# The first two units of a chunked attention kernel: another load order, other PSUM banks, and one hand-over at a time

## The chip, the core and the metric

The kernel runs on one core of a Trainium2 chip. The metric is device time in microseconds (us) of one execution. Six parts matter here: PE (TensorE, matrix multiplies), DVE (VectorE), ACT (ScalarE), POOL (GpSimd), SP (SyncE, which here only issues DMA transfers) and the DMA engines. Each engine works through its own list of instructions in order, and semaphores tie the lists together.

## What is computed

A linear attention with a decaying state, per batch and head, and behind it two feed-forward layers:

```
for t in range(S):                                    # S = 768, D = 48, 4 batches, 8 heads
    y[:, :, t] = r_t @ (state + (u * k_t) v_t)
    state      = w_t[:, None] * state + k_t v_t
x   = y as [3072 tokens, 384]
x   = max(x @ w_in, 0) ** 2 @ w_out                   # 384 -> 2048 -> 384
out = ((x @ w_a) * (x @ w_b)) @ w_out2                # 384 -> 1536 -> 384
```

## The kernel before

The 768 steps are cut into 6 chunks of 128, so that there are 24 units (a chunk of one batch), numbered chunk by chunk. For a unit, `load_unit` fetches four tiles: `lw` (decays), `lkr` (k and r, transposed), `vn` (v) and `nn` (k and r with tokens on partitions). `prepare` turns decays into factors on DVE (two scans at L197 and L202, four products at L206 to L210), while POOL multiplies `nn` with `u` (tile `u_bc`) and with itself (L220, L221); DVE sums that up to `dd` (L223), and ACT builds a diagonal `A` from it (L226, eight instructions). `scores` lets PE multiply k with r into two PSUM tiles `ps` (L239, four matmuls each) and transpose k into `pt` (L243); its `post` copies the scores over `A` under a mask on DVE (L247, two copies) and takes `pt` out on ACT (L250). `mix` lets PE multiply `A` with v into `py` (L267) and k with v into `pk` (L274); its `post` copies `py` to SBUF on ACT (L284), shifts it with six small DMAs (L287) and updates the state on DVE (L292, L294).

Units 0 and 1 make the first tile of tokens, 256 wide. The first layer then runs over it in 16 steps (L414): three matmuls into `hp` (L417), a relu on ACT (L423), a product on DVE (L424, tile `g`), and, two steps later, three matmuls into `acc` (L410). `hp` has two PSUM buffers, so that the third `hp` step waits for the first product. Weights come packed: `decode` takes two ACT and two DVE instructions a tile (L41 to L44), and `split_w1` parts the decoded tile into a high and a low half for the later, 512 wide tiles (L144, L145). In those each step is nine matmuls into `hp` and nine into `acc` (L311 to L313), with a product at L464 and a split at L372 on DVE. The attention of later units, the decoding and the splits run between these steps.

The program's text is not the order in which the engines work. A scheduler builds each engine's list from the data that instructions need, from priorities and from its own timeline; `high_priority(offset=HP)` pulls work ahead. So an edit to the first two units moves instructions of other units too. PSUM's eight banks are in three pools: `p_acc` (3, the layer's sums), `p_mm` (2, `hp`) and `p_at` (3, attention).

Of the kernel before, what the change touches and what calls it, by code (L numbers as in the profile page):

```python
# [8 lines left out]
F32 = mybir.dt.float32  # L9
# [7 lines left out]
B, H, S, D = 4, 8, 768, 48  # L17
# [3 lines left out]
C = 128  # L21
# [3 lines left out]
G = 4  # L25
GP = 112
T = B * C
HP = 100
# [43 lines left out]
def chunked_path(ctx, tc, flags, krT, wT, krn, vn, u, w1, w2, w3, w4, w5, out):  # L72
    nc = tc.nc
    pe, act, dve, pool, sync = nc.tensor, nc.scalar, nc.vector, nc.gpsimd, nc.sync
# [8 lines left out]
    at = ctx.enter_context(tc.tile_pool(name="at", bufs=1))  # L83
    dr = ctx.enter_context(tc.tile_pool(name="dr", bufs=1, space=bass.MemoryType.DRAM))
    p_acc = ctx.enter_context(tc.tile_pool(name="p_acc", bufs=3, space=PS))
    p_mm = ctx.enter_context(tc.tile_pool(name="p_mm", bufs=2, space=PS))
    p_at = ctx.enter_context(tc.tile_pool(name="p_at", bufs=3, space=PS))
# [82 lines left out]

    loaded = {}

    def load_unit(i):
        b, c = units[i]
        w = ld.tile([GP, G * (C + 1) + 1], F32, tag="lw", name="lw")
        kr = ld.tile([GP, 2, G, C], F32, tag="lkr", name="lkr")
        v = ld.tile([128, H, D], F32, tag="vn", name="vn", bufs=3)
        nn = ld.tile([128, 2, H, D], F32, tag="nn", name="nn")
        r0 = b * S + c * C
        sync.dma_start(out=w, in_=wT[b, c])  # L180
        sync.dma_start(out=kr, in_=krT[b, c])
        sync.dma_start(out=v, in_=vn[r0:r0 + C].rearrange("p (h d) -> p h d", h=H))
        sync.dma_start(out=nn, in_=krn[r0:r0 + C].rearrange("p n (h d) -> p n h d", h=H))
        loaded[i] = w, kr, v, nn

    xt = {}
    tiles = [(0, 1)] + [tuple(range(i, i + 4)) for i in range(2, NU - 2, 4)] + [(NU - 2, NU - 1)]
# [3 lines left out]
    def prepare(i):  # L191
        b, c = units[i]
        w, kr, v, nn = loaded.pop(i)
        k, r = kr[:, 0], kr[:, 1]
        fq = at.tile([GP, 2, G * (C + 1)], F32, tag="f", name="fq")
        f, q = (fq[:, n].rearrange("p (g t) -> p g t", g=G) for n in range(2))
        dve.tensor_tensor_scan(  # L197
            out=fq[:, 0], data0=w[:, :-1], data1=d1.rearrange("p g t -> p (g t)"),
            initial=0.0, op0=ALU.mult, op1=ALU.max,
        )  # L200
        dve.reciprocal(out=d2[:, :, C:], in_=f[:, :, C:])
        dve.tensor_tensor_scan(  # L202
            out=fq[:, 1, ::-1], data0=w[:, 1:][:, ::-1], data1=d2.rearrange("p g t -> p (g t)")[:, ::-1],
            initial=0.0, op0=ALU.mult, op1=ALU.add,
        )
        dve.tensor_tensor(out=r, in0=r, in1=f[:, :, 0:C], op=ALU.mult)  # L206
        e = w[:, 0:G * C].rearrange("p (g t) -> p g t", g=G)
        dve.tensor_tensor(out=k, in0=k, in1=q[:, :, 1:], op=ALU.mult)
        dve.tensor_tensor(out=e, in0=f[:, :, 1:], in1=q[:, :, 1:], op=ALU.mult)
        dve.scalar_tensor_tensor(  # L210
            out=k, in0=e, scalar=2.0, in1=k, op0=ALU.subtract, op1=ALU.mult, reverse0=True
        )
        pe2 = at.tile([GP, G, 2, 1], F32, tag="pe2", name="pe2", bufs=2)
        dve.tensor_tensor(
            out=pe2[:, :, :, 0], in0=f[:, :, C:C + 1].to_broadcast([GP, G, 2]),
            in1=half.to_broadcast([GP, G, 2]), op=ALU.mult,
        )
        act.activation(out=fq, in_=fq, func=AF.Square, accum_out=chk[:, i:i + 1])
        p = nn[:, 0]
        pool.tensor_tensor(out=p, in0=p, in1=u_h, op=ALU.mult)  # L220
        pool.tensor_tensor(out=p, in0=p, in1=nn[:, 1], op=ALU.mult)  # L221
        dd = at.tile([128, H, 1], F32, tag="dd", name="dd", bufs=2)
        dve.tensor_reduce(out=dd[:, :, 0], in_=p, axis=AX.X, op=ALU.add)  # L223
        A = at.tile([128, 2, G, C], F32, tag="A", name="A", bufs=2)
        for h in range(H):
            act.activation(out=A[:, h % 2, h // 2, :], in_=ident, func=AF.Copy, scale=dd[:, h])  # L226
        unit[i] = dict(k=k, r=r, v=v, A=A, pe2=pe2)
        if i + 2 < NU:
            load_unit(i + 2)

    def scores(i):

        b, c = units[i]
        st = unit[i]
        ps = [p_at.tile([128, G, C], F32, tag="at", name="ps") for _ in range(2)]
        for g in range(G):
            for j in range(2):
                s = slice(64 * j, 64 * j + D)
                pe.matmul(out=ps[j][:, g, :], lhsT=st["k"][s, g, :], rhs=st["r"][s, g, :], start=True, stop=True)  # L239
        if c < NC - 1:  # L240
            pt = p_at.tile([128, 4, C], F32, tag="at", name="pt")
            for g in range(G):
                pe.transpose(out=pt[:, g, 0:GP], in_=st["k"][:, g, :], identity=ident[:GP, :GP])  # L243

        def post():
            for j in range(2):
                dve.copy_predicated(st["A"][:, j], mask.bitcast(I32).to_broadcast([128, G, C]), ps[j])  # L247
            if c < NC - 1:
                st["kt"] = at.tile([128, G, GP], F32, tag="kt", name="kt")
                act.activation(out=st["kt"], in_=pt[:, :, 0:GP], func=AF.Copy)  # L250
        return post

    def mix(i):

        b, c = units[i]
        st = unit.pop(i)
        A, v, s = st["A"], st["v"], states[b]
        ps = p_at.tile([128, G, C], F32, tag="at", name="py")
        if c > 0:
            for g in range(G):  # L260
                pe.matmul(
                    out=ps[0:GP, g, :], lhsT=s[:, g].rearrange("p j d -> p (j d)")[:, 0:GP],
                    rhs=st["r"][:, g, :], start=(g == 0), stop=False, skip_group_check=True,
                )
        for g in range(G):
            for j in range(2):
                pe.matmul(  # L267
                    out=ps[64 * j:64 * j + D, g, :], lhsT=v[:, 2 * g + j, :], rhs=A[:, j, g, :],
                    start=(c == 0), stop=True, skip_group_check=True,
                )  # L270
        if c < NC - 1:
            pk = p_at.tile([128, G, 2, D], F32, tag="at", name="pk")
            for g in range(G):
                pe.matmul(out=pk[0:GP, g], lhsT=st["kt"][:, g, :], rhs=v[:, 2 * g:2 * g + 2, :], start=True, stop=True)  # L274

        def post():
            if i > 1:
                x = at.tile([128, G, C], F32, tag="x", name="xf", bufs=2)
            else:
                if i == 0:  # L280
                    x0[0] = xp.tile([128, G, 2, C], F32, tag="x", name="x0")
                x = x0[0][:, :, i, :]
            for rows in ((slice(0, GP),) if c > 0 else (slice(0, D), slice(64, GP))):
                act.activation(out=x[rows], in_=ps[rows], func=AF.Copy)  # L284
            for p0 in (0, 64):
                for m in range(3):
                    sync.dma_start(out=x[p0 + 48:p0 + 64, m], in_=x[p0 + 16 * m:p0 + 16 * m + 16, 3])  # L287
            if c < NC - 1:
                src = pk[0:GP]
                if c > 0:  # L290
                    t = at.tile([GP, G, 2, D], F32, tag="kt", name="t")
                    dve.tensor_tensor(out=t, in0=src, in1=s[:, :, :, 0:D], op=ALU.add)  # L292
                    src = t
                dve.tensor_tensor(  # L294
                    out=s[:, :, :, 0:D], in0=src, in1=st["pe2"].to_broadcast([GP, G, 2, D]), op=ALU.mult
                )
            return (lambda: split_x(i, x)) if i > 1 else None
        return post
# [14 lines left out]
        pe.matmul(out=out, lhsT=wt[:, 1, sl], rhs=rhs_hi, start=False, stop=last)  # L313


    load_unit(0)
    make_identity(nc, ident)
    for s in states:
        pool.memset(s, 0.0)
# [2 lines left out]
        out=mask, in_=mask, pattern=[[0, 1], [1, 128]], compare_op=ALU.is_gt, fill=0.0, base=0, channel_multiplier=-1  # L322
# [7 lines left out]
    dve.memset(half[0:64, :, 0:1], 1.0)  # L330
    dve.memset(half[64:GP, :, 1:2], 1.0)
    sync.dma_start(out=u_bc, in_=u.rearrange("h d -> (h d)").rearrange("(o n) -> o n", o=1).to_broadcast([128, DM]))
    load_unit(1)
    load_w1(2)
    tails = []
    with tc.high_priority(offset=HP):
        prepare(0)
    for i in range(2):
        with tc.high_priority(offset=HP):
            p = scores(i)  # L340
            if i == 0:
                prepare(1)
            p()
            mix(i)()
        decode_w1()
        decode_w1()

# [56 lines left out]
    acc = [p_acc.tile([128, N], F32, tag="acc", name="acc") for _ in range(3)]  # L404
# [9 lines left out]
    for f in range(16):  # L414
        hp = p_mm.tile([128, N], F32, tag="mm", name="hp")
        for k in range(3):
            pe.matmul(  # L417
                out=hp, lhsT=w_in[f][:, k * 128:(k + 1) * 128],
# [22 lines left out]
    for n in range(1, len(tiles)):  # L441
# [4 lines left out]
        acc = [p_acc.tile([128, N], F32, tag="acc", name="acc") for _ in range(3)]  # L446
# [281 lines left out]
```

## Time and profile before

| | us |
|---|---|
| median of 3 runs (lowest to highest) | 1030.02 (1028.35 to 1032.36) |
| the profiled execution | 1029.76 |
| its span in the trace | 1028.1 |
| PE busy | 984.1 (96%) |
| DVE busy | 540.5 (53%) |
| ACT busy | 448.3 (44%) |
| POOL busy | 72.7 (7%) |

The span is 1.66 us shorter than the execution's own time. PE is busy in 96% of the span, so 44.0 us are all that its idle time comes to. The shares of the whole span hide where that lies: the page's 40 slices, the waits and the timeline of the first 260 us tell it. A busy PE is not a PE at full speed: the duration of a matmul of one shape has to be looked at beside it.

### The profile page before, as it was taken

To read this page: it belongs to the slowest core of one execution; us is meant where nothing else is said; L and a number is where in the kernel's file an instruction comes from. 1 tells how busy PE (TensorE), PEld (TensorE's weight loads), DVE (VectorE), ACT (ScalarE), POOL (GpSimd) and SP (SyncE) were. 2 spreads that over 40 slices of the span, in tenths; PEclk is the share of its full clock that TensorE was granted. 3 is DMA by queue.
4 is the path that set the end of the run, shared out by engine and by line. 5 is a ranking of instruction groups with operands and counts; after the bars stand their busy time and mean duration, and the time that the engine had idled before them with its cause. 6 is when DMAs were issued, how large, how long until landed. Compare 5 with 4: busy or idle time off the path is not lost. (4 is left out here: it accounts for less than half of the span.)

```text
span 1028.1 us, 13834 instructions
## 1 busy us (share of the span) xinstructions
PE 984.1 (96%) x5250; PEld 834.4 (81%) x5250; DVE 540.5 (53%) x908; ACT 448.3 (44%) x930; POOL 72.7 (7%) x60
## 2 busy tenths in 40 slices
PE   3789999998999999999999999999999999999996
PEld 2577777777788888887889988888888888888885
DVE  8999999988856756644346622222222222222221
ACT  5788676777555444543336612222322312212211
POOL 4234201000100100000000000000000000000000
PEclk9999999999999999999999999999999999999998
DMA  9677237877422221201015400100100100000001
GB/s 274 218 254 244 67 95 254 258 257 244 146 83 64 77 67 54 65 21 54 23 46 155 132 1 2 61 1 21 41 1 1 41 1 16 27 1 32 0 1 34
DMA packets 47020, 88.15 MB, mean 86 GB/s; under 512 B 7008, under 2 KB 25568, under 8 KB 46944
## 3 DMA queue, kind: packets, MB, share of 16 engines
q1 hardware_dynamic: 40464, 77.74, 24.5%
q10 hardware_dynamic: 6480, 9.44, 2.6%
q8 instruction: 43, 0.70, 0.3%
q14 instruction: 33, 0.27, 0.1%
HBM read 69.46 MB, written 16.52 MB: 84 GB/s over the span
## 5 line engine op out<-in xcount | busy, mean ns | idle before, releaser
L536 DVE TENSOR_TENSOR t<-ap,t 128x512 f32<-128x512 f32 x72 | 49.8, 691 | 278.7 <-PE ap L313 278.7
L371 ACT ACTIVATE gh<-t 128x512 fp32r<-128x512 f32 (+1 forms) x168 | 102.4, 609 | 185.3 <-DVE t L536 127.0
L372 DVE TENSOR_TENSOR gl<-t,gh 128x512 fp32r<-128x512 f32 (+1 forms) x168 | 112.1, 667 | 74.7 <-ACT gh L371 74.4
L527 ACT ACTIVATE t<-bp 128x512 f32<-128x512 f32 x72 | 43.1, 598 | 160.4 <-PE bp L313 159.7
L311 PE MATMUL hp<-x,w 128*128 128x512 f32 (+1 forms) x288 | 109.3, 379 | 2.7 <-DVE t L464 2.7
L312 PE MATMUL acc<-gl,w 128*128 128x512 f32 (+1 forms) x288 | 108.2, 376 | 1.9 <-DVE gl L372 1.8
L313 PE MATMUL acc<-gh,w 128*128 128x512 f32 (+1 forms) x288 | 107.5, 374 | 0.0
L312 PE MATMUL hp<-x,w 128*128 128x512 f32 (+1 forms) x288 | 107.2, 372 | 0.0
L313 PE MATMUL hp<-x,w 128*128 128x512 f32 (+1 forms) x288 | 107.1, 372 | 0.0
L311 PE MATMUL acc<-gh,w 128*128 128x512 f32 (+1 forms) x288 | 102.6, 383 | 0.0
L464 DVE TENSOR_TENSOR t<-t,hp 128x512 f32<-128x512 f32 (+1 forms) x96 | 61.0, 635 | 74.0 <-ACT t L463 74.0
L518 PE MATMUL acc<-w,gh 128*128 128x384 f32 x288 | 96.8, 336 | 0.0
L519 PE MATMUL acc<-w,gh 128*128 128x384 f32 x288 | 96.7, 336 | 0.0
L520 PE MATMUL acc<-w,gl 128*128 128x384 f32 x288 | 95.1, 337 | 0.0
L463 ACT ACTIVATE t<-hp 128x512 f32<-128x512 f32 (+1 forms) x96 | 53.3, 555 | 83.2 <-PE hp L313 81.3
L313 PE MATMUL bp<-x,w 128*128 128x512 f32 x216 | 85.3, 395 | 0.0
L312 PE MATMUL bp<-x,w 128*128 128x512 f32 x216 | 85.1, 394 | 0.0
L312 PE MATMUL ap<-x,w 128*128 128x512 f32 x216 | 84.1, 390 | 0.0
L313 PE MATMUL ap<-x,w 128*128 128x512 f32 x216 | 84.1, 389 | 0.0
L311 PE MATMUL ap<-x,w 128*128 128x512 f32 x216 | 84.1, 389 | 0.0
L311 PE MATMUL bp<-x,w 128*128 128x512 f32 x216 | 83.8, 390 | 0.0
L311 PEld LDWEIGHTS hp<-x,w 128*128 128x128 f32 x288 | 54.2, 188 | 14.4 <-DVE t L464 4.3
(93 smaller groups left out, 1713.5 us busy)
## 6 DMA issues: line engine op xcount, KB each, us to landing
raw<-in_w SPq DMA_DIRECT2D x68, 384.0 KB, 4.7
lkr<-in_krT SPq DMA_DIRECT2D x24, 448.0 KB, 4.1
nn<-in_krn SPq DMA_DIRECT2D x24, 384.0 KB, 3.9
w2d<-f SPq DMA_DIRECT2D x36, 192.0 KB, 2.8
ws<-w2d SPq DMA_DIRECT2D x36, 192.0 KB, 2.5
lw<-in_wT SPq DMA_DIRECT2D x24, 226.2 KB, 3.4
vn<-in_vn SPq DMA_DIRECT2D x24, 192.0 KB, 2.8
out<-e ACTq DMA_DIRECT2D x24, 192.0 KB, 1.9
```

Source lines behind the costliest of these rows:

```text
L311: pe.matmul(out=out, lhsT=wt[:, 0, sl], rhs=rhs_hi, start=first, stop=False)
L312: pe.matmul(out=out, lhsT=wt[:, 0, sl], rhs=rhs_lo, start=False, stop=False)
L313: pe.matmul(out=out, lhsT=wt[:, 1, sl], rhs=rhs_hi, start=False, stop=last)
L371: act.activation(out=gh, in_=t, func=AF.Copy)
L372: dve.tensor_tensor(out=gl, in0=t, in1=gh.bitcast(F32), op=ALU.subtract)
L463: act.activation(out=t, in_=hp, func=AF.Relu)
L464: dve.tensor_tensor(out=t, in0=t, in1=hp, op=ALU.mult)
L518: pe.matmul(out=acc[t], lhsT=ph[:, sl], rhs=w_o[f][:, 0, :], start=(f == 0), stop=False)
L519: pe.matmul(out=acc[t], lhsT=ph[:, sl], rhs=w_o[f][:, 1, :], start=False, stop=False)
L520: pe.matmul(out=acc[t], lhsT=pl[:, sl], rhs=w_o[f][:, 0, :], start=False, stop=(f == 11))
L527: act.activation(out=bs, in_=bp, func=AF.Copy)
L536: dve.tensor_tensor(out=bs, in0=ap, in1=bs, op=ALU.mult)
```

## The change

Three edits, all for units 0 and 1. First, their loads are issued in another order: `lw`, `lkr`, then `u_bc`, then `nn` ahead of `vn`. All other units too now load `nn` ahead of `vn`. Second, `scores` and `mix` take their PSUM tiles from a pool that is given: unit 0 has `p_at` for its scores and `p_mm` for its mix, unit 1 has `p_acc` (three banks) for its scores and `p_at` for its mix. Third, the loop prepares, scores and mixes unit 0 in full, and then unit 1; before, unit 1 was prepared between unit 0's scores and their post.

```
-    def load_unit(i):
+    def load_unit(i, late=None):
...
-        sync.dma_start(out=v, in_=vn[r0:r0 + C].rearrange("p (h d) -> p h d", h=H))
-        sync.dma_start(out=nn, in_=krn[r0:r0 + C].rearrange("p n (h d) -> p n h d", h=H))
+        def rest():
+            sync.dma_start(out=nn, in_=krn[r0:r0 + C].rearrange("p n (h d) -> p n h d", h=H))
+            sync.dma_start(out=v, in_=vn[r0:r0 + C].rearrange("p (h d) -> p h d", h=H))
+
         loaded[i] = w, kr, v, nn
+        if late is None:
+            rest()
+        else:
+            late.append(rest)
...
-    def scores(i):
+    def scores(i, pool=None, tag="at"):
...
-    def mix(i):
+    def mix(i, pool=None, tag="at"):
...
-    load_unit(0)
+    late = []
+    load_unit(0, late)
...
-    load_unit(1)
+    late[0]()
+    load_unit(1, late)
+    late[1]()
     load_w1(2)
     tails = []
-    with tc.high_priority(offset=HP):
-        prepare(0)
     for i in range(2):
         with tc.high_priority(offset=HP):
-            p = scores(i)
-            if i == 0:
-                prepare(1)
-            p()
-            mix(i)()
+            prepare(i)
+            scores(i, *((p_at, "at"), (p_acc, "acc"))[i])()
+            mix(i, *((p_mm, "mm"), (p_at, "at"))[i])()
         decode_w1()
         decode_w1()
```

In the changed file lines stand 6 to 9 further down (L197 is L203, L247 is L254, L424 is L431, L464 is L471, L239 is L246, L267 is L275, L274 is L282); L145 stays. The engines' lists differ from the 19th DVE instruction and the 23rd PE instruction on. They are the same again in the last 769 of 1221 on DVE and the last 4015 of 4887 on PE; POOL's list has the same order throughout.

The first place is PE behind the mix of unit 0. In both lists `ps` are scores, `pt` the transposed k, `py` and `pk` the two products of the mix. Before:

```order
L267 MATMUL py<-A,vn 48x128 x8
L274 MATMUL pk<-vn,kt 112x96
L239 MATMUL ps<-lkr 128x128 x4
L274 MATMUL pk<-vn,kt 112x96 x3
L239 MATMUL ps<-lkr 128x128 x4
L243 MATMUL pt<-ident,lkr 128x112 x4
```

And of the changed kernel:

```order
L275 MATMUL py<-A,vn 48x128 x8
L282 MATMUL pk<-vn,kt 112x96 x4
L246 MATMUL ps<-lkr 128x128 x8
L250 MATMUL pt<-ident,lkr 128x112 x4
```

Unit 1's scores no longer come in two groups of four, one for each `ps` tile; the eight now take turns between the two tiles.

The second place is DVE ahead of the first product of the 256 wide tile (`g`). Here `lw`, `lkr` and `fq` belong to `prepare` of a later unit, `A` to a copy of scores, `wf` to decoding, `s` to a state. Before:

```order
L197 SCALAR_TENSOR_TENSOR fq<-lw,d_133 112x516
L44 SCALAR_TENSOR_TENSOR wf<-raw,wf 128x384 x3
L201 RECIPROCAL d_135<-fq 112x4
L206 TENSOR_TENSOR lkr<-lkr,fq 112x512
L42 SCALAR_TENSOR_TENSOR wf<-raw 128x384
L202 SCALAR_TENSOR_TENSOR fq<-lw,d_135 112x516
L42 SCALAR_TENSOR_TENSOR wf<-raw 128x384
L424 TENSOR_TENSOR g<-g,hp 128x256 x2
```

And of the changed kernel:

```order
L214 TENSOR_TENSOR lkr<-lkr,fq 112x512
L215 TENSOR_TENSOR lw<-fq 112x512
L302 TENSOR_TENSOR s_141<-pk,pe_372 112x8x48
L42 SCALAR_TENSOR_TENSOR wf<-raw 128x384
L44 SCALAR_TENSOR_TENSOR wf<-raw,wf 128x384
L254 COPY_PREDICATED A<-mask,ps 128x512
L216 SCALAR_TENSOR_TENSOR lkr<-lw,lkr 112x512
L220 TENSOR_TENSOR pe_677<-fq,half 112x8
L254 COPY_PREDICATED A<-mask,ps 128x512
L42 SCALAR_TENSOR_TENSOR wf<-raw 128x384
L431 TENSOR_TENSOR g<-g,hp 128x256
```

The first product has moved back behind unit 3's two copies of scores and behind the rest of a `prepare`.

The third place is DVE between the last product of that tile and the first product of the 512 wide one (`t<-t,hp`); `w<-wf,w` is a split of a weight. Before:

```order
L424 TENSOR_TENSOR g<-g,hp 128x256
L145 TENSOR_TENSOR w<-wf,w 128x384 x3
L247 COPY_PREDICATED A<-mask,ps 128x512 x2
L201 RECIPROCAL d_135<-fq 112x4
L206 TENSOR_TENSOR lkr<-lkr,fq 112x512
L214 TENSOR_TENSOR pe_1424<-fq,half 112x8
L145 TENSOR_TENSOR w<-wf,w 128x384 x4
L202 SCALAR_TENSOR_TENSOR fq<-lw,d_135 112x516
L464 TENSOR_TENSOR t<-t,hp 128x512
```

And of the changed kernel:

```order
L431 TENSOR_TENSOR g<-g,hp 128x256
L145 TENSOR_TENSOR w<-wf,w 128x384 x3
L214 TENSOR_TENSOR lkr<-lkr,fq 112x512
L215 TENSOR_TENSOR lw<-fq 112x512
L145 TENSOR_TENSOR w<-wf,w 128x384 x4
L216 SCALAR_TENSOR_TENSOR lkr<-lw,lkr 112x512
L203 SCALAR_TENSOR_TENSOR fq<-lw,d_133 112x516
L471 TENSOR_TENSOR t<-t,hp 128x512
```

The copies, the first scan's followers and seven splits that stood behind these products before now stand ahead of the last narrow product, and the wide product has the end of that `prepare` and the first scan of the next one ahead of it.

## Rows read from the trace of the kernel before

**Rows 1.** The page: busy us with share and count; DVE's busy tenths in 40 slices.

```profile
PE 984.1 (96%) x5250; PEld 834.4 (81%) x5250; DVE 540.5 (53%) x908; ACT 448.3 (44%) x930; POOL 72.7 (7%) x60
...
DVE  8999999988856756644346622222222222222221
```

**Rows 2.** Windows: stretch, length, busy PE, PEld, DVE, ACT, POOL; PEclk, DMA share, GB/s.

```profile
120.00:130.00 10.00, 9.06 (x61) 7.54 (x60) 10.00 (x20) 8.63 (x21) 0.02 (x1) 1.00 0.14 44
...
160.00:200.00 40.00, 40.00 (x196) 30.73 (x194) 37.36 (x64) 30.73 (x64) 7.03 (x4) 1.00 0.77 251
200.00:300.00 100.00, 94.09 (x528) 74.97 (x529) 81.20 (x140) 63.33 (x134) 10.71 (x8) 1.00 0.60 190
```

**Rows 3.** Timeline of the start: start us, duration us, engine, line, operation, idle before.

```profile
3.77 1.23 DVE L197 TENSOR_TENSOR_SCAN fq<-lw,d 112x516 f32<-112x516 f32 x1 [1.51 <-DMA lw<-in_wT]
...
9.05 2.08 PE L239 MATMUL ps<-lkr 48*128 48x128 f32 x16 [9.05 <-DVE lkr L210]
...
9.50 0.99 POOL L220 TENSOR_TENSOR nn<-nn,u_bc 128x384 f32<-128x384 f32 x1 [5.80 <-DMA u_bc<-in_u]
...
10.63 2.03 DVE L197 TENSOR_TENSOR_SCAN fq<-lw,d 112x516 f32<-112x516 f32 x1 [1.63 <-DMA lw<-in_wT]
...
22.39 2.07 PE L239 MATMUL ps<-lkr 48*128 48x128 f32 x8
```

**Rows 4.** Timeline around the first product of the 256 wide tile.

```profile
43.50 3.78 PE L417 MATMUL hp<-x,wf 128*128 128x256 f32 x8
...
53.52 0.73 DVE L424 TENSOR_TENSOR g<-g,hp 128x256 f32<-128x256 f32 x2
...
53.98 1.56 PE L417 MATMUL hp<-x,wf 128*128 128x256 f32 x6 [1.06 <-DVE g L424]
...
59.26 0.55 PE L243 MATMUL pt<-ident,lkr 112*128 112x112 f32 x4
...
59.74 1.08 PE L267 MATMUL py<-A,vn 128*48 128x128 f32 x16
...
64.57 0.94 PE L274 MATMUL pk<-vn,kt 128*112 128x96 f32 x8
...
65.43 1.16 PE L239 MATMUL ps<-lkr 48*128 48x128 f32 x8
```

**Rows 5.** Timeline at the first product of the 512 wide tile.

```profile
125.83 0.65 DVE L464 TENSOR_TENSOR t<-t,hp 128x512 f32<-128x512 f32 x1
...
126.53 0.50 PE L311 MATMUL hp<-x,w 128*128 128x512 f32 x1 [0.94 <-DVE t L464]
```

**Rows 6.** DVE by line and shape, 0 to 160 us: count, busy us, mean ns, idle.

```profile
L42 DVE SCALAR_TENSOR_TENSOR wf<-raw 128x384 int32<-128x384 int32 x32 | 19.1, 610 | 0.0
L145 DVE TENSOR_TENSOR w<-wf,w 128x384 fp32r<-128x384 f32 x32 | 18.3, 603 | 0.0
L44 DVE SCALAR_TENSOR_TENSOR wf<-raw,wf 128x384 int32<-128x384 int32 x32 | 16.9, 547 | 0.0
L197 DVE TENSOR_TENSOR_SCAN fq<-lw,d 112x516 f32<-112x516 f32 x11 | 15.0, 1365 | 3.1 <-DMA lw<-in_wT 3.1
...
L247 DVE COPY_PREDICATED A<-mask,ps 128x512 f32<-128x512 int32 x20 | 14.2, 723 | 0.0
L208 DVE TENSOR_TENSOR lkr<-lkr,fq 112x512 f32<-112x512 f32 x11 | 9.3, 845 | 0.0
L209 DVE TENSOR_TENSOR lw<-fq 112x512 f32<-112x512 f32 x10 | 9.2, 919 | 0.0
...
L210 DVE SCALAR_TENSOR_TENSOR lkr<-lw,lkr 112x512 f32<-112x512 f32 x10 | 6.8, 678 | 0.1
```

**Rows 7.** Timeline of PE, 195 to 260 us: every start with a wait.

```profile
230.41 0.50 PE L312 MATMUL acc<-gl,w 128*128 128x512 f32 x1 [1.60 <-DVE gl L372]
...
244.83 1.16 PE L239 MATMUL ps<-lkr 48*128 48x128 f32 x12 [2.60 <-ACT xf L284]
...
253.84 0.50 PE L311 MATMUL hp<-x,w 128*128 128x512 f32 x1 [0.49 <-DVE t L464]
```

More of the change, by code (lines that the diff above doesn't have):

```diff
@@ L229, in prepare @@
             load_unit(i + 2)
-    def scores(i):
+    def scores(i, pool=None, tag="at"):
         b, c = units[i]
         st = unit[i]
-        ps = [p_at.tile([128, G, C], F32, tag="at", name="ps") for _ in range(2)]
+        pool = pool or p_at
+        ps = [pool.tile([128, G, C], F32, tag=tag, name="ps") for _ in range(2)]
         for g in range(G):
@@ L240, in scores @@
         if c < NC - 1:
-            pt = p_at.tile([128, 4, C], F32, tag="at", name="pt")
+            pt = pool.tile([128, 4, C], F32, tag=tag, name="pt")
             for g in range(G):
@@ L257, in mix @@
         A, v, s = st["A"], st["v"], states[b]
-        ps = p_at.tile([128, G, C], F32, tag="at", name="py")
+        pool = pool or p_at
+        ps = pool.tile([128, G, C], F32, tag=tag, name="py")
         if c > 0:
@@ L271, in mix @@
         if c < NC - 1:
-            pk = p_at.tile([128, G, 2, D], F32, tag="at", name="pk")
+            pk = pool.tile([128, G, 2, D], F32, tag=tag, name="pk")
             for g in range(G):
```

## The prediction

> **What bounds the kernel now.** I read the page's shares first: PE is busy for 984.1 us of a span of 1028.1, so an edit that leaves PE's work alone can only add to or take from 44.0 us of idle time [rows 1]. The slices say when another engine matters: DVE is at nine tenths or more in slices 2 to 8, which is 26 to 206 us, at eight in the next three, and at two to seven tenths later, when PE's work alone counts [rows 1]. The windows sharpen that: from 120 to 130 us DVE is busy for 10.00 of 10 and PE for 9.06; from 160 to 200 PE for all 40; from 200 to 300 DVE has fallen to 81.20 of 100 [rows 2]. So there are three stretches. Up to 43 us PE waits for the first two units. From 43 to about 150 us both engines are close to full, and since DVE has hardly a gap, the moment at which a DVE result is there is given by how much DVE work stands ahead of it in its list. From then on PE sets the pace. The lists of the two kernels are the same in the last 4015 PE instructions, of 4887, so whatever the change does, it does ahead of those, and they are moved as one block.
>
> **The loads.** In the start, the scan of unit 1 at 10.63 us takes 2.03 us, the same scan of unit 0 at 3.77 took 1.23 [rows 3]. Beside the slow one runs the pair of POOL products that begins at 9.50, when `u_bc` has landed [rows 3]. `u_bc` and `nn` now go ahead of `vn`, so the pair starts earlier and overlaps the idle 1.63 us in which DVE waits for unit 1's decays [rows 3]. Those decays have the same bytes ahead of them as before, so the wait itself stays. I take 2.03 - 1.23 = 0.80 us off DVE's start. The bounds are 0 (POOL's pair merely disturbs something else) and 1.35, since one decode instruction of 0.547 [rows 6] has also left the place ahead of unit 1's second copy.
>
> **The banks.** Unit 0's scores take 2.08 us for 16 pieces, when the two tiles take turns; of unit 1, one tile's 8 pieces alone took 2.07 [rows 3], and its list has two such groups. With two free banks the eight matmuls take turns again, so PE saves some 2.07 us. I count that at nothing: what follows on PE, `py` of unit 1, needs DVE's masked copies, and these have the same DVE work ahead of them as before but for that one instruction. If the copies were early, it would be worth up to 2.07.
>
> **One by one.** This is the edit that moves most, since the scheduler now lays out DVE's list anew. I count by kind what DVE has ahead of a given product in the new list and not in the old.
>
> Ahead of the first product of the 256 wide tile: one L208, L209, L210, L42 and L44 each and two copies L247, which with the mean durations is 0.845 + 0.919 + 0.678 + 0.610 + 0.547 + 2 x 0.723 = 5.05 us [rows 6] (two short instructions more are left out). That product began at 53.52 and PE's third `hp` step, which needs its buffer, at 53.98 after a wait of 1.06 [rows 4]. It will come 5.05 - 0.80 = 4.25 us later, at about 57.8. PE has more to do by then: four transposes, four scores, four `pk` and eight `py`, 0.55 + 1.16 + 0.94 + 1.08 = 3.73 us [rows 4]. But the `py` among them need unit 3's two copies, which now stand three and five instructions ahead of the product. So most of this extra work can't fill the gap, and PE waits in one piece of some 3.5 us: PE ran out at 53.98 - 1.06 = 52.92 [rows 4], less 0.80 and plus 0.55 of transposes, and the first of the two copies ends about 1.5 us before the product starts.
>
> Ahead of the first product of the 512 wide tile: one L197, L208, L209 and L210 each and seven splits L145: 1.365 + 0.845 + 0.919 + 0.678 + 7 x 0.603 = 8.03 us [rows 6]. There was no slack here: the product ended at 125.83 + 0.65 = 126.48, and the `hp` step that needs its buffer began at 126.53 [rows 5]. Of PE's work only four `pk` more are done by then, 0.94 us [rows 4]. So PE stands behind by 8.03 - 0.80 - 0.94 = **6.29 us** with equal work done. The loss at the first product is contained in this and is not added. The lists of the next steps bring it no lower at once (ahead of the fifth such product DVE still has about 6 us more to do), and PE has no gap between 160 and 200 us in which to catch up [rows 2].
>
> **What comes back.** What DVE did early it need not do late. Between 200 and 260 us PE waits 1.60, 2.60 and 0.49 us, 4.69 in all [rows 7]. With PE some 6 us later the ACT, DVE and DMA work that ended these waits has that much more time. I give back the 2.60 (ACT's copy of `py`) and the 0.49, and keep the 1.60: the split it waits for still has about 6 us more DVE work ahead of it in the new list. That is 3.09, with bounds of 0 and 4.69.
>
> The sum against the profiled execution: 1029.76 + 6.29 - 3.09 = 1032.96, so **1033 us**. That execution lies 0.26 us under the median of the three runs, which I leave in the rounding. About 0.5% (5.1 us) is what a measurement of this kernel can tell from no change.
>
> **Rivals.**
>
> *The loss stays.* If none of the late waits goes, since ACT and DVE are just as late as PE, the time is 1029.76 + 6.29 = 1036. For it: the new list keeps more DVE work ahead of each step for some twenty steps. Against it: DVE's 81% from 200 to 300 us [rows 2] leaves it room.
>
> *PE's clock falls again.* The eight pieces at 43.50 take 3.78 us, six of the same shape at 53.98 take 1.56 [rows 4]: 0.47 against 0.26 each, so PE ran at the lower of its two levels until about 50 us, though the granted clock reads 1.00 in the windows [rows 2]. The new wait of 3.5 us falls right behind the change of level. If PE drops back, the work behind it takes up to twice as long, at most 10.6 us more for what lay between 53.98 and 64.57 [rows 4]; part of that hides in PE's waits for DVE, and I put 4 us on it, with bounds of 0 and 10.6: 1037. Against it: the 12 pieces of scores behind the 2.60 us wait at 244.83 took 1.16 us [rows 7], no sign of a lower level. The Trainium skill, in "TensorE: Matmul & The Clock Gate", section "HAM oscillation — how this bites in real kernels", warns that a PE left idle between bursts of matmuls goes back to its half-rate clock and starts the next burst slowly. By that rule this rival would be the forecast; the trace has no idle stretch of over 3 us after the level rose, so it can't say.
>
> *The start decides (the other sign).* If the instructions ahead of the products are filler that PE's slack absorbs, what remains is the start, 1.35 us, and the late waits, 4.69: 1029.76 - 6.04 = 1024. It needs the products to be no later than before, that is, DVE to get through its list about 6 us sooner than the mean durations say. For it: those means hold stretches beside POOL (1.365 for a scan that alone takes 1.23 [rows 3, 6]), and PE begins unit 0's mix earlier. Against it: DVE has no slice under nine tenths from 26 to 206 us [rows 1], and POOL has the same work in the same order.
>
> *Nothing happens.* The work moved early is done within waits that are there anyway, and the time stays at 1030.
>
> **How the numbers follow.** Forecast, a loss partly given back, 0.45; the loss stays, 0.22; the clock, 0.05; the start decides, 0.20; nothing, 0.08. Slower by over 0.5% are the loss that stays and the clock: 0.27. Faster by over 0.5% is the start: 0.20. Within 0.5%: 0.53. The range reaches down to the start's 1024 and up to 1038, just over the two slower cases. The likeliest case alone spans 1028 to 1036: 1.35 instead of 0.80 at the start and all 4.69 back give 1030.8, less what shorter DVE durations would bring; nothing back gives 1036.
>
> **What would show it.** The first product at L431 should start at 57 to 59 us and PE have a wait of 3 to 4 us just before unit 3's `py`; earlier than 55 speaks for the start. The first product at L471 should start at about 133 us, with DVE full until then; the third 512 wide `hp` step should begin some 6 us later than its 126.53. Between 200 and 260 us PE's waits should come to some 1.6 us; 4 or more speak for the loss that stays. Pieces of 0.47 us behind the long wait would be the clock. The forecast is wrong if DVE shows gaps before 120 us, for then the counting of its list doesn't hold, or if the stretch from 300 us on has another length than before.

## The result, and the profile of the changed kernel

The changed kernel takes 1040.34 us (median of 12 runs), the kernel before 1030.29 in the same comparison; the ratio is 1.0084, 95% interval [1.0067, 1.0101]. It is slower by 0.8%, outside the predicted range. Its profiled execution took 1038.07 us, 8.31 more than the profiled execution before, and its span is 1036.3.

The page of the changed kernel (first line: busy us with share and count; then the granted clock in tenths, 40 slices):

```profile
PE 991.2 (96%) x5250; PEld 841.7 (81%) x5250; DVE 538.4 (52%) x908; ACT 449.4 (43%) x930; POOL 73.2 (7%) x60
...
PEclk9989999998999999999999999999999999999999
```

PE's busy time has grown by 7.1 us [rows 1], its idle time from 44.0 to 45.1: the loss shows as slower matmuls more than as waits. The clock's row has two slices below nine tenths ahead of the end, where the kernel before has none. The timeline of PE in the changed kernel tells where (start us, duration us, line, shape, idle before and what ended it):

```profile
44.11 2.07 PE L424 MATMUL hp<-x,wf 128*128 128x256 f32 x4 [2.27 <-DMA x<-x]
...
53.13 0.60 PE L250 MATMUL pt<-ident,lkr 112*128 112x112 f32 x4 [0.44 <-DVE s L302]
54.71 0.42 PE L275 MATMUL py<-A,vn 128*48 128x128 f32 x2 [0.97 <-DVE A L254]
56.34 1.81 PE L282 MATMUL pk<-vn,kt 128*112 128x96 f32 x8 [1.22 <-ACT kt L257]
...
61.96 2.93 PE L424 MATMUL hp<-x,wf 128*128 128x256 f32 x6
...
99.51 2.65 PE L424 MATMUL hp<-x,wf 128*128 128x256 f32 x6 [1.96 <-DVE g L431]
...
133.27 0.50 PE L319 MATMUL hp<-x,w 128*128 128x512 f32 x1 [0.74 <-DVE t L471]
...
207.42 0.47 PE L319 MATMUL hp<-x,w 128*128 128x512 f32 x1 [0.38 <-DVE t L471]
...
225.13 0.50 PE L319 MATMUL acc<-gh,w 128*128 128x512 f32 x1 [1.85 <-ACT ev L405]
...
244.30 1.19 PE L269 MATMUL py<-lkr,s 112*112 112x128 f32 x4 [4.03 <-ACT kt L257]
...
293.21 0.39 PE L319 MATMUL hp<-x,w 128*128 128x512 f32 x1
...
548.23 0.50 PE L319 MATMUL bp<-x,w 128*128 128x512 f32 x1
```

The same late places in the kernel before (the 17th and the 31st 512-wide `hp` step and the first matmul of the second layer; the row at 271.71 is a wait that the changed kernel doesn't have):

```profile
199.49 0.49 PE L311 MATMUL hp<-x,w 128*128 128x512 f32 x1
...
271.71 0.50 PE L311 MATMUL hp<-x,w 128*128 128x512 f32 x1 [1.22 <-DVE t L464]
...
283.25 0.39 PE L311 MATMUL hp<-x,w 128*128 128x512 f32 x1
...
538.27 0.50 PE L311 MATMUL bp<-x,w 128*128 128x512 f32 x1
```

The third 512-wide `hp` step is 133.27 - 126.53 = 6.74 late [rows 5]. By then the changed kernel's PE has done the four `pk` more that the prediction named, 0.94 us, so that 5.80 us of lateness compare with the 6.29 that it counted for equal work. Step by step the lateness goes up and down after that, since the two lists of PE have the attention at other places. At the 17th step both have done the same matmuls again, and it is 207.42 - 199.49 = 7.93. At the 31st it is 293.21 - 283.25 = 9.96, and at the second layer 548.23 - 538.27 = 9.96 too. From there to PE's last matmul both need 480.45 us, and the end after it happened to be 1.7 us shorter. So some 5.8 us are lost up to the third step, 2.1 from there to the 17th and 2.0 from there to the 31st; on balance nothing comes back.

The windows of PE in the changed kernel (busy us, count, granted clock, DMA share, GB/s) show the clock:

```profile
50.00:60.00 10.00, 7.37 (x55) 0.77 0.80 243
60.00:70.00 10.00, 10.00 (x40) 0.72 0.77 249
...
240.00:250.00 10.00, 5.97 (x18) 0.66 0.60 207
```

PE fell to the lower of its two levels during the waits of 0.44, 0.97 and 1.22 us, which follow each other closely, again after the 1.96 and the 1.85 and during the 4.03, some 24 us in all. The step at 61.96 took 2.93 us for six pieces that took 1.56 before [rows 4].

### The profile page after: what moved, and what is told of

Same layout as the page of the kernel before. It is cut to its first block, busy times and chain, and to the rows that moved or that the text cites. A ratio compares the mean times of both kernels' runs of the same rounds, so it can differ in the third digit from the quotient of the medians.

```text
span 1036.3 us, 13840 instructions
## 1 busy us (share of the span) xinstructions
PE 991.2 (96%) x5250; PEld 841.7 (81%) x5250; DVE 538.4 (52%) x908; ACT 449.4 (43%) x930; POOL 73.2 (7%) x60
## 5 line engine op out<-in xcount | busy, mean ns | idle before, releaser
L319 PE MATMUL acc<-gh,w 128*128 128x512 f32 (+1 forms) x288 | 103.3, 383 | 1.8 <-ACT ev L405 1.8
L471 DVE TENSOR_TENSOR t<-t,hp 128x512 f32<-128x512 f32 (+1 forms) x96 | 61.1, 636 | 76.9 <-ACT t L470 76.7
```

The costliest lines, as they stand in the source:

```text
L319: pe.matmul(out=out, lhsT=wt[:, 0, sl], rhs=rhs_hi, start=first, stop=False)
L471: dve.tensor_tensor(out=t, in0=t, in1=hp, op=ALU.mult)
```

## The experiments

"Step" is the start of the third 512-wide `hp` step, "to layer 2" the time from it to the first `bp` matmul; both are from each run's profile, the times from all its runs. Each ratio is to runs of the kernel before in the same comparison, whose medians were 1029.0 to 1031.2. Executions of one kernel differ: e3_handover has every engine's list of the kernel before, and its step came 1 us later and its second layer 1.2 us earlier.

| run | median us | ratio, 95% interval | step | to layer 2 |
|---|---|---|---|---|
| before | 1030.29 | 1 | 126.53 | 411.7 |
| changed | 1040.34 | 1.0084 [1.0067, 1.0101] | 133.27 | 415.0 |
| e1_loads | 1034.76 | 1.0050 [1.0031, 1.0068] | 131.59 | 412.8 |
| e2_banks | 1031.66 | 1.0019 [1.0003, 1.0035] | 126.03 | 418.3 |
| e3_handover | 1030.00 | 1.0012 [0.9998, 1.0027] | 127.51 | 409.6 |
| e4_order_of_before | 1030.79 | 0.9995 [0.9978, 1.0012] | 129.61 | 410.9 |
| e5_order_of_after | 1038.40 | 1.0070 [1.0047, 1.0093] | 133.23 | 413.6 |
| e6_after_filled | 1039.84 | 1.0094 [1.0071, 1.0117] | 133.04 | 415.7 |
| e7_before_warm | 1032.45 | 1.0013 [1.0000, 1.0025] | 129.79 | 409.1 |
| e8_before_less | 1030.61 | 1.0013 [1.0002, 1.0025] | 126.56 | 411.3 |
| e9_after_less | 1036.97 | 1.0056 [1.0035, 1.0077] | 132.51 | 414.7 |
| e10_before_more | 1040.76 | 1.0109 [1.0093, 1.0126] | 137.44 | 409.0 |
| e11_vector_list | 1054.04 | 1.0242 [1.0220, 1.0265] | 133.40 | 428.3 |
| e12_before_to_62 | 1039.77 | 1.0094 [1.0069, 1.0118] | 133.36 | 413.5 |
| e13_after_to_72 | 1033.15 | 1.0020 [1.0002, 1.0037] | 129.72 | 410.4 |
| e14_before_to_127 | 1040.72 | 1.0092 [1.0067, 1.0117] | 129.08 | 421.1 |
| e15_after_to_133 | 1037.24 | 1.0053 [1.0035, 1.0071] | 134.34 | 414.8 |
| e16_more_loads | 1035.40 | 1.0047 [1.0029, 1.0064] | 134.09 | 412.9 |
| e17_fewer_loads | 1031.68 | 1.0011 [0.9995, 1.0027] | 130.41 | 410.2 |
| e18_fewer_both | 1030.28 | 1.0002 [0.9987, 1.0017] | 126.31 | 413.0 |

### Which of the three edits

Each edit alone, on the kernel before:

```
e1_loads:     load_unit(0, late) ... late[0](); load_unit(1, late); late[1]()      # nn ahead of vn
e2_banks:     scores(1, p_acc, "acc"), mix(0, p_mm, "mm")
e3_handover:  for i in range(2): prepare(i); scores(i)(); mix(i)()
```

> Only the other order of the first loads; banks and hand-over as before. With it VectorE's list is planned anew: the products L424 stand behind 4.0 to 10.4 us more VectorE work than before, the 512-wide products L464 behind 3.0 to 7.9 us more (in the changed kernel 5.8 to 12.0 and 7.5 to 12.6). Theory 'list' (a product that stands later on VectorE's list makes TensorE wait, at the full clock): the third wide step about 4.4 - 0.9 = 3.5 us later than before, total 1033 to 1035, granted clock full after 49 us. Theory 'clock' (the new waits of TensorE ahead of the first products drop its clock, and half-rate stretches cost as much again): stretches at a granted clock near 0.5 after 50 us, as in the changed kernel, total 1036 to 1040. If the loads are harmless: 1029 to 1031.

> Only the other PSUM banks for the attention of the first two units; loads and hand-over as before. The plan moves the products the other way: L424 stand behind 4.8 to 15.5 us less VectorE work than before, the first wide products L464 behind 3.5 to 10.5 us less; the masked copies L247 of units 6 to 9 stand 3 to 10 us later. Theory 'list': waits for products go (1.06 at 53.98 and 0.94 at 126.53 in the kernel before), and what is late is the copies, ahead of py; total 1027 to 1030. Theory 'clock': with fewer waits ahead of the products no half-rate stretch between 50 and 130 us; total as before or less, 1026 to 1030. If the banks are what costs the time in the changed kernel: 1036 to 1040.

> Only the hand-over of each unit in full, one by one; loads and banks as before. The built kernel has the same instructions in the same order on every engine as the kernel before. Both theories: 1030, ratio 1.000 within 0.002. The prediction, which booked the late products on the hand-over, would say 1033 to 1036.

The hand-over alone changes nothing: the lists of all engines are the same with and without it, and so is the time. The loads cost 0.5%; that is the total which theory 'list' named, but the granted clock fell too (0.76 from 50 to 60 us), so that the run doesn't decide between the two theories. The banks put the products 5 to 15 us earlier on DVE's list, and the step came no earlier (126.03); the time is 0.2% up, above what both theories said (1030 at most), with 418.3 us behind the step. That loads and banks together, without the hand-over, make the changed kernel's lists is what remains; no run has these two alone with a plan of their own.

### The edits or the order

Order constraints between neighbours of one engine hold its list as it is in the other kernel:

```
 flag = chunked_path(...)
+keep_order(tc, ("DVE", "PE", "Activation", "Pool"))
```

> The changed loads and banks, with the instructions of TensorE, VectorE, ScalarE and GpSimd held in the order that they have in the kernel before. Theory 'order' (the loads and the banks cost nothing by themselves; the new plan costs the time): 1028 to 1031, third wide step at 126 to 127.5. If the loads or the banks cost by themselves, in the queue or at the banks: 1034 to 1040.

> The loads and banks of before, with the instructions of the same four engines held in the order that they have in the changed kernel. Theory 'order': 1037 to 1042, third wide step at 132 to 134, half-rate stretches of TensorE as in the changed kernel. If the loads or the banks cost by themselves: 1028 to 1032.

With the old order the new loads and banks cost nothing, and gain nothing either: 0.9995. With the new order the old loads and banks are as slow as the changed kernel. **The order of the instructions carries the whole loss.** SP's list of transfers was not held in these two runs, but it came out within some ten of 393 transfers of the list in the kernel whose order the other engines have; so its order counts as part of this.

### TensorE's clock

```
+fillers(tc, pe, acc[0][:, 384:512], ident, mask[:, 0, :], [(pt, 2), (py, 5), (pk, 6), (hp, 10)])      # e6, on the changed kernel
+fillers(tc, pe, warm[:, 0:128], ident, mask[:, 0, :], [(ps, 22), (py, 40), (pt, 36), (pk, 8), (py, 30)])   # e7, on the kernel before
```

> The changed kernel in its own order, with 23 additional matmuls whose output nobody reads, in TensorE's waits at 52.7, 53.7, 55.1 and 97.5 us (2, 5, 6 and 10 of them, 128 columns each, 0.15 us at the full clock). Theory 'list' (VectorE's list sets the products, a slow TensorE in between is hidden by the wait for them): the granted clock stays full from 49 to 110, the third wide step comes at 132 to 134 all the same, total 1036 to 1040. Theory 'clock' (the half-rate stretches cost it): clock full from 49 to 110, third wide step at 128 to 130, total 1033 to 1036. If the clock falls in spite of the added matmuls, the waits are not what drops it.

> The kernel before in its own order, with 136 additional matmuls whose output nobody reads, in TensorE's waits of the first 43 us (22 ahead of the first scores, 40 ahead of unit 0's py, 36 and 8 ahead of unit 1's pt and pk, 30 ahead of unit 2's py). In the kernel before TensorE's matmuls take the time of the half clock until 49 us, some 27 us of them. Both: the clock rises ahead of 20 us instead of at 49. Theory 'list' (VectorE is busy throughout from 50 to 170 and sets the pace): what TensorE gains it waits, third wide step no earlier than 125.5, total 1028 to 1031. Theory 'clock' (slow matmuls add to the time): the third wide step at 115 to 121, total 1018 to 1024.

PE's windows in e6_after_filled and its third narrow and third wide step:

```profile
50.00:60.00 10.00, 9.56 (x87) 1.00 0.86 266
60.00:70.00 10.00, 8.62 (x50) 1.00 0.83 255
...
100.00:110.00 10.00, 10.00 (x71) 1.00 0.35 111
```

```profile
60.33 1.56 PE L464 MATMUL hp<-x,wf 128*128 128x256 f32 x6
...
133.04 0.50 PE L355 MATMUL hp<-x,w 128*128 128x512 f32 x1 [0.80 <-DVE t L511]
```

The added matmuls kept the clock at its upper level (1.00 where the changed kernel has 0.77 and 0.72), and the narrow step at 60.33 ran at full rate. Yet the wide step came at 133.04 and the time is no better: what PE gained it waited later, or spent on the 23 additional matmuls themselves. In e7_before_warm PE was busy throughout from 3.75 to 30 us and at full clock from 9.5 us on instead of 49, but for 3.4 us at half rate near 58. That gained nothing:

```profile
10.00:20.00 10.00, 10.00 (x97) 1.00 1.03 308
20.00:30.00 10.00, 10.00 (x92) 1.00 0.66 209
```

Its fillers ran 4.9 us too long ahead of the first `hp` step (48.4 for 43.5), so its step (129.79) has that lateness in it; by "clock" it should have come at 115 to 121, or at 120 to 126 with the lateness added. So up to the third wide step the slow matmuls fill time in which PE would have waited: they are how the loss looks, not its cause. Behind 200 us neither run tests the clock: in e6_after_filled it fell there as well, to 0.83 from 210 to 220 and from 240 to 250 us.

### How much work VectorE has

```
-dve.scalar_tensor_tensor(out=fi, in0=high, scalar=3, in1=fi, ...)       # e8, e9: in the first 14 decodes
+dve.tensor_tensor(out=pad, in0=d1[:, 0:3, 0:128], in1=..., op=ALU.max)  # e10: 14 times, ahead of the first product
+keep_order(tc, ("DVE",))                                                # e11: the order of before
```

> The kernel before in its own order, without the second of VectorE's two instructions in the first 14 weight decodes (left out of the computation: the exponents of those weights); 14 x 0.55 = 7.7 us less VectorE work ahead of the third wide step. Theory 'VectorE's list sets the pace to 130': the step goes down from 126.5 as far as TensorE's own work allows, that is by its waits after 43 us, 6.4 us at most; total 1024 to 1027. Theory 'TensorE's own order sets it': 1028 to 1030.

> The changed kernel in its own order, without the same 14 instructions. Theory 'VectorE's list': the third wide step back from 133.3 to 126 to 128, total 1030 to 1034 (all of the loss gone: 1031; if the last 3 us belong to the order after the step, 1034). Theory 'TensorE's own order': step at 131 or later, total 1036 to 1040.

> The kernel before in its own order, with 14 additional VectorE instructions of 112x384 (about 0.55 us each, 7.7 us; their output is read by nobody) ahead of the first product. Both theories of the place: the third wide step 7.7 - 0.9 = 6.8 us later, at about 133. If part of a lateness comes back in the later waits, as the prediction booked (3.09 of it): total 1033 to 1034.5. If nothing comes back: 1036 to 1038. If lateness grows by the clock: 1039 or more.

> The changed loads and banks with VectorE's instructions alone held in the order of the kernel before; the other engines are planned anew. Theory 'VectorE's list': 1029 to 1032, third wide step at 126 to 128. If the other engines' new order carries the loss: 1035 to 1040.

My second theory, that VectorE's work sets the pace all the way up to 130 us, fell: with 7.7 us less of it the step stayed at 126.56 and at 132.51 (the ratio of e9_after_less, 1.0056, is lower than the 1.0084 of the changed kernel, but the intervals overlap). In both kernels the first 14 decodes are over by 69 us, though, so that these two runs say nothing of the work that stands on the list later. The windows of e8_before_less (PE, PEld, DVE, ACT, POOL) and DVE's waits from 43 to 133 us (us in total, times, longest) say what took its place:

```profile
60.00:70.00 10.00, 9.92 (x64) 8.27 (x59) 6.12 (x11) 8.78 (x22) 2.01 (x2) 1.00 0.89 239
```

```profile
DVE lkr L239 <- DMA lkr<-in_krT: 3.3, 1, 3.3
DVE dd L256 <- ACT A L259: 1.0, 1, 1.0
```

DVE now stands idle for 3.9 us of ten, waiting for a unit's load and then for ACT. Additional work delays the step by its full length. The 14 instructions of e10_before_more took 11.02 us in all (DVE's timeline, first): ten took the expected 0.55 to 0.57 us, four 1.23 to 1.25, while products ran on POOL (54.03 to 59.88 us). PE waited for the product behind them (PE's timeline, second):

```profile
54.68 11.02 DVE L368 TENSOR_TENSOR pad<-d 112x384 f32<-112x384 f32 x14
```

```profile
66.08 2.50 PE L451 MATMUL hp<-x,wf 128*128 128x256 f32 x5 [12.43 <-DVE g L458]
...
137.44 0.50 PE L338 MATMUL hp<-x,w 128*128 128x512 f32 x1 [0.97 <-DVE t L498]
...
546.48 0.50 PE L338 MATMUL bp<-x,w 128*128 128x512 f32 x1
```

For 11.0 us of work the step is 10.9 us late. The expectation counted 7.7 us, so its times are too low. What the run was to decide stays open: in the profiled execution the second layer is 546.48 - 538.27 = 8.2 us late, so that 2.7 us came back behind the step; but that was the fastest of five runs (1037.95 us), and over all five the time is up by 1.09%, 11.2 us.

VectorE's list alone in the old order, with the other lists planned anew around it, is the worst of all. A list is good or bad only together with the others.

### Where in the order

The order of one kernel up to a step, that of the other behind it:

```
 keep_order(tc, (...))     # e12: before to 61.9, then changed    e13: changed to 72.0, then before
                           # e14: before to 126.5, then changed   e15: changed to 133.3, then before
```

> The changed loads and banks; on TensorE, VectorE, ScalarE and GpSimd the order of the kernel before up to its fifth narrow hp step (61.9 us there), from there the order of the changed kernel. Theory 'start' (the loss is made between 44 and 72, where unit 3's attention stands ahead of the third narrow step): third wide step at 126 to 129; total 1030 to 1032, or 1033 to 1034 if the order of after costs another 3 behind the step. If the loss is spread over the order: 1034 to 1038.

> The converse: the order of the changed kernel up to its fifth narrow hp step (72.0 us there), from there that of the kernel before. Theory 'start': third wide step at 132 to 135; total 1036 to 1039. If the loss is made later: 1030 to 1033.

> The changed loads and banks; the order of the kernel before up to its third 512-wide hp step (126.5 us there), from there that of the changed kernel. Theory 'late order' (3 of the 10 us belong to the order behind the step): step at 126 to 130, total 1033 to 1035. If those 3 us are only the lateness carried on: 1029 to 1032.

> The converse: the order of the changed kernel up to its third 512-wide hp step (133.3 us there), from there that of the kernel before. Theory 'late order': step at 132 to 134, total 1035 to 1037. If the lateness itself costs the 3 us behind the step: 1038 to 1040. If it comes back there, as the prediction booked: 1032 to 1034.

I had put the loss between 44 and 72 us, at unit 3's attention. That fell as well: with the old start and the new order from 62 us on the step is at 133.36 (first row), with the new start and the old order from 72 on at 129.72 (second row, another kernel).

```profile
133.36 0.48 PE L346 MATMUL hp<-x,w 128*128 128x512 f32 x1
```

```profile
129.72 0.50 PE L346 MATMUL hp<-x,w 128*128 128x512 f32 x1 [0.94 <-DVE t L502]
```

Over all runs the step lies at 126.3 to 130.4 wherever the old order rules from 72 us to the step and no work was added, and at 132.5 to 134.3 wherever the new one does. The totals of e12_before_to_62 and e14_before_to_127 lie outside all that was expected of them, and e15_after_to_133 (1037.24) just above the first of its own cases. The seam at 127 costs much by itself (421.1 us behind it), so e14_before_to_127 does not show what the new tail costs alone; e15_after_to_133 lies between the two kernels.

The last column tells more on the 3 us behind the step: with the old order throughout it is 409.0 to 413.0 (nine kernels, mean 410.9), with the new one 413.6 to 415.7 (four kernels, mean 414.7), and a lateness of 10.9 us in e10_before_more makes it no longer (409.0). I read from this that these 3.8 us belong to the order there and not to the lateness; e15_after_to_133 (414.8) speaks against it, though it has a seam at the step. The profiles place most of it between the third and the 17th step: 72.9 to 73.4 us in the nine, 74.2 to 78.2 in the four. From the 17th to the 31st step both groups spread alike, 80.7 to 85.0 and 81.5 to 85.8 us.

### The stream of weights

In both kernels the weights of the first layer are decoded by the same time. DVE in the kernel before, the last second-half decode (L44) and the last narrow product:

```profile
109.83 1.01 DVE L44 SCALAR_TENSOR_TENSOR wf<-raw,wf 128x384 int32<-128x384 int32 x2
...
117.77 0.41 DVE L424 TENSOR_TENSOR g<-g,hp 128x256 f32<-128x256 f32 x1
```

And in the changed kernel, with the first and the last product at L431, and the product ahead of the step:

```profile
57.58 0.41 DVE L431 TENSOR_TENSOR g<-g,hp 128x256 f32<-128x256 f32 x1
...
110.20 0.55 DVE L44 SCALAR_TENSOR_TENSOR wf<-raw,wf 128x384 int32<-128x384 int32 x1
...
126.01 0.39 DVE L431 TENSOR_TENSOR g<-g,hp 128x256 f32<-128x256 f32 x1
126.32 1.48 DVE L145 TENSOR_TENSOR w<-wf,w 128x384 fp32r<-128x384 f32 x3
127.73 0.68 DVE L214 TENSOR_TENSOR lkr<-lkr,fq 112x512 f32<-112x512 f32 x1
128.33 0.68 DVE L215 TENSOR_TENSOR lw<-fq 112x512 f32<-112x512 f32 x1
128.93 1.95 DVE L145 TENSOR_TENSOR w<-wf,w 128x384 fp32r<-128x384 f32 x4
130.81 0.68 DVE L216 SCALAR_TENSOR_TENSOR lkr<-lw,lkr 112x512 f32<-112x512 f32 x1
131.41 1.22 DVE L203 TENSOR_TENSOR_SCAN fq<-lw,d 112x516 f32<-112x516 f32 x1
132.56 0.66 DVE L471 TENSOR_TENSOR t<-t,hp 128x512 f32<-128x512 f32 x1
```

The decodes end at 110.84 and 110.75; the last narrow product starts 8.24 us later in the changed kernel. VectorE as a whole is not behind, the products are behind on it: the new order has let preparation and splits of later tiles go first.

These rows hold the cause of the late third step. From the end of the last decode to the first wide product, for which PE waits at that step, DVE is busy without a gap in both kernels. In the old order 26 instructions stand between the two and take 14.99 us (110.84 to 125.83, [rows 5]); in the new order there are 39, and they take 21.81. The difference of 6.8 us is the lateness. The other profiles have the same two lengths: where DVE has no gap there, it is 14.96 to 14.99 us with the old order (nine profiles, e10, e13, e14 and e17 among them) and 21.80 to 21.82 with the new one (the changed kernel, e5, e6, e12 and e15). When the last decode ends is another matter, and the same in both kernels. In all profiles it ends 10.5 to 13.1 us after the last of these weights has landed (at 99.4 us before, 99.3 changed). Three runs changed the stream:

```
+sync.dma_start(out=dr.tile([128, 768], I32), in_=src[f])        # e16: eight times
-sync.dma_start(out=nn, in_=krn[r0:r0 + C]...)                   # e17, e18: units 3 to 7
-dve.scalar_tensor_tensor(out=fi, in0=high, scalar=3, ...)       # e18: first 14 decodes
```

> The kernel before in its own order, with 8 additional transfers of 0.39 MB (copies of weight blocks that nobody reads), spread over SP's queue between the 11th and the 26th weight load. Theory 'stream' (all profiles have the last weight load landed at 98.7 to 102.7 and the last decode done at 110 to 114, whatever was changed; that stream sets the pace to there, and what VectorE's list holds behind it decides the rest): 3.1 MB at 250 to 300 GB/s are 10 to 12 us more; last weight load lands at 105 to 111, third wide step at 132 to 138, total 1034 to 1042. If the loads have slack: 1029 to 1032.

> The kernel before in its own order, without the loads of nn (krn) for units 3 to 7, which use the tile of an earlier unit instead (left out of the computation: those units' own k and r rows in the diagonal term); 2.0 MB or some 7 us of stream less. Theory 'stream and VectorE, both full': no gain, VectorE is busy throughout from 50 to 170; third wide step at 125 to 127, total 1028 to 1031. If the loads alone set the pace: step at 119 to 122, total 1022 to 1026.

> The same, and without the 14 VectorE instructions of the run with less VectorE work, which alone gained nothing. Theory 'stream and VectorE, both full': now there is a gain; last weight load at 92 to 97, third wide step at 119 to 124, total 1023 to 1027. If neither sets the pace: 1028 to 1031, step at 126.

More loads make it slower, and PE waits for it just where the last weights come in e16_more_loads:

```profile
107.03 1.22 PE L448 MATMUL hp<-x,wf 128*128 128x256 f32 x2 [4.28 <-DVE g L455]
```

Fewer loads, even with less VectorE work, gain nothing: the step is at 130.41 in e17_fewer_loads, later than either expectation, and at 126.31 in e18_fewer_both. But these two runs did not bring the weights in sooner: the last of them landed at 103.3 us in the one and at 98.6 in the other, for which 92 to 97 was expected. SP issues all loads in one order, and a unit's load waits until its buffer is free. SP's waits in the kernel before, from 0 to 110 us (us in total, times, longest):

```profile
SPq L180 <- DVE lkr L210: 10.6, 4, 3.8
SPq L181 <- PE py L261: 7.3, 1, 7.3
```

So what sets the time at which the last weights land, and with it the end of the last decode (109 to 118 us, and 122 in e10), is **still open**: DVE and PE free the buffers on which the loads wait, and the loads feed DVE. What is shown is the rest: 6.8 us more on DVE's list between the last decode and the first wide product.

## Why the prediction was wrong

**The step that failed is "what comes back".** The sum gave back 3.09 of 6.29 us, because DVE has room from 200 to 300 us. On balance nothing came back: measured where PE has done the same work, the lateness is 5.80 us at the third wide step, 7.93 at the 17th and 9.96 from the 31st to the end. The waits of 1.60, 2.60 and 0.49 us [rows 7] did go, and so did the 1.22 at 271.71, but others came: 0.38, 1.85 and 4.03, which is 6.26 us for 5.91, and 10.2 us at half rate with them. That is the sign (4 us or more) that the prediction had named for the loss that stays. I read those waits as the ends of chains through ACT and DVE that are planned as late as PE, so that a later PE does not find them done; no run shows this by itself. Where the old order was held, in e10_before_more, 2.7 of 10.9 us did come back in the profiled execution, about what the sum had booked. With nothing given back the sum is 1036.05; the rival "the loss stays", at 0.22, was nearer than the forecast. Of the loss behind the third step, 2.1 us lie between it and the 17th, where the prediction saw no term; PE waits there for 0.85, 0.55 and, just ahead of the 17th, the 0.38 us (before: 0.16 and 0.12), which is 1.5 us more. The rest does not show as waits, and I can't name it, nor say which part of the last 2.0 us is the clock.

**The lateness at the third wide step was right in mechanism and size**, 5.80 for 6.29 with equal work done, and the first product came at 57.58 for "57 to 59". The eleven instructions that the prediction counted at 8.03 us by the durations of [rows 6] are the ones that stand between 126.32 and 132.56 in the new order; they took 6.24 us, and two narrow products more stand ahead of them. Its reading, so much work ahead, so much later, holds behind the last decode, where DVE has no gap. Ahead of it the reading fails: 7.7 us less work there became idle time for the most part (4.9 us from 43 to 100 us in e8_before_less) and did not bring the step forward (e8, e9), since the last decode ended no earlier than before (110.9 us) in e8 and only 1.5 us earlier in e9. DVE also had two gaps between 43 and 120 us, 0.9 and 0.6 us, which the prediction had named as a sign against its counting; they did not upset it.

**The edit was the wrong one.** The text booked the new list on the hand-over; e3_handover has the old list. What remains as its origin are the loads and the banks. That cost the sum nothing, but someone who had undone the hand-over would have found nothing.

**The start** gave nothing for the 0.80: the scan of unit 1 took 1.28 us, as hoped, but waited 2.34 for its decays, not 1.63 [rows 3], and ended at 12.64 instead of 12.66. e4_order_of_before has the early loads without the new order, and gains nothing. The banks saved PE the 2.07 us, as the prediction had it (unit 1's 16 pieces of scores took 2.08 us), and they were worth nothing, as it counted: PE then waited 5.75 us ahead of unit 1's mix.

**The clock** was a rival at 0.05, priced at 4 us. Its sign came: half rate behind the waits ahead of unit 3's attention, though these were three short ones and not one of 3.5 us. Its price was wrong up to the third wide step: with the clock kept up there the time is the same (e6). The rule of the Trainium skill in "TensorE: Matmul & The Clock Gate", section "HAM oscillation — how this bites in real kernels", that a PE idle between bursts falls to half rate, agrees with the 4.03 us wait: the granted clock is 0.66 from 240 to 250 us. Up to the third wide step the half rate cost nothing here, because PE would have waited for DVE's product otherwise (in e6_after_filled the step came at 133.04 with the clock up); for the stretch behind 200 us no run shows what it cost.

**The range** ended at 1038 since no case let anything grow behind the third wide step. The stretch from 300 us on has the same length in both kernels, as the prediction had it.

## What to carry to other kernels

Where a scheduler plans all engines from one text, an edit costs or gains first by the new plan: build each edit alone, compare the lists, and price those. To tell an edit from its plan, keep the old order and apply the edit. A wait that you expect to shrink because its waiter comes later need not shrink when the work that ends it is planned later too; and a slow matmul or a busy engine is a cause only if relieving it moves the next fixed point in the program. The relief has to lie in the right place: work taken from a full engine ahead of the last thing that it waits for becomes idle time, and only what stands behind that counts. To find the place, go back from the late instruction to the last one that both kernels reach at the same time.

## What the runs showed of the hardware

- The granted clock fell behind a single wait of 1.96 us and behind one of 1.85, and during 0.44, 0.97 and 1.22 close together, but not behind one of 2.60 in the kernel before [rows 7]. It also differs between executions: e3_handover, with the same lists, was at half rate for 6.8 us behind 243 us, where the kernel before had 1.00.
- The clock's record starts with its first rise: until then the windows read 1.00 while matmuls take the time of half rate, 0.47 us a piece for 0.26 [rows 4]. Where PE was kept busy from 3.75 us on (e7) that rise came at 9.5 us, otherwise at 22 to 50.
- VectorE's 112x384 instructions with two operands in SBUF took 0.57 us while POOL was idle and 1.23 to 1.25 us from 55.3 to 60.3 us, while products ran on POOL (e10_before_more).
